# A new order for the ramp, products of zeros in its gaps, and six steps moved behind attention steps

## The chip, the cores and the metric

The kernel runs on one core of a Trainium2 chip. Its engines are TensorE (PE in the profile, with its weight loads as PEld), VectorE (DVE), ScalarE (ACT), GpSimd (POOL) and the queue of SyncE (SP), which issues nearly all DMAs. The metric is the device time of one execution in microseconds. Kernel before: 889.75 us, the median of three runs (886.77, 889.75 and 893.33).

## What is computed

Three layers follow each other on 3,072 tokens of 512 features: chunked attention, a gated two-matrix layer, and a layer with softmax and layer norm. The weights of the two later layers come as float64.

```python
# attention: 32 queries see 16 left, 32 own, 8 right keys and 8 memory keys
scores = scale * np.matmul(q_c, k_full.transpose(0, 1, 3, 2))
scores = scores - np.max(scores, axis=-1, keepdims=True)
a = np.exp(scores)
a = a / (np.sum(a, axis=-1, keepdims=True) + 1e-09)
out[:, :, c_start:c_end] = np.matmul(a, v_full)
# layer 1
x = (x @ w_a) * (x @ w_b) @ w_out
# layer 2
h = x @ w_in
e = np.exp(h - h_max)
solu = h * e / (np.sum(e, axis=-1, keepdims=True) + 1e-09)
return (solu - mu) / np.sqrt(var + 1e-06) * g_ln @ w_out
```

## The kernel before

**Products.** Each operand of the large products is kept as two parts, a high one rounded to the fast float32 format of TensorE and a low one with the rest; a product is then three products (`mm3`, lines 857 to 859) of 128x512. The attention's own products (64-row pieces, 64 or 32 columns) are plain float32.

**Attention groups.** 128 queries of all eight heads are one group, in eight steps: P makes the tile `s` (two of the eight banks of PSUM), S (line 194) is the product of queries and keys, 64 small products in the trace; M (205, 206) takes off the row maximum on DVE; X (214) is the exponential on ACT into `EB`; N (222 to 225) normalises, in the first stage on DVE; T (235) transposes on TensorE into `pt`, and a copy on ACT (237) brings that into `AT`; V (259) multiplies with the values; a copy on ACT (273, the high part of `x`) and a subtraction on DVE, L (278, the low part), end it. Later, pairs of groups do the same in one (`pair_P` to `pair_V`, lines 304 to 372; 128 small products in S and in V).

**Weights.** A layer-1 weight column block f (f = 0 to 11) comes as float64 words (`raw`, 1.5 MB) and is turned into its two parts by seven steps: abs and low on ACT (378, 381), range and sign and add on DVE (391, 392, 399, 407), hi on ACT (410), lo on DVE (414).

**Stages.** The first 40 us, the ramp, do the four groups of the first 512 tokens and turn weight blocks 0 to 2. Then a loop over f runs block 0: two runs of 12 products (`ab`) with a copy to `G` (1323), the gate on DVE and ACT (872, 874, 878), 12 products into `acc`, and the turning of weight blocks f+1 to f+3 between them. A second loop over f runs block 1. The four blocks left go two by two with seven half-size products in place of eight; the sums of weights that this takes are made in the second loop (`s1_whole`, `s1_sums`, `s1_hi`, `s1_lo`: lines 488, 502, 513, 520, on DVE, DVE, ACT, DVE) and, for `w_out`, in the third (`wo_load` to `wo_store`: 622, 632, 636, 640, 643). Layer 2 comes last, from 410 us on.

**What sets the order.** PE, DVE and ACT run in the order in which the code is written, one instruction after the other. In the ramp that is the list of calls at lines 1237 to 1291. In the first loop it is `plan`, whose numbers name a place ("9b" is behind the gate of f = 9; 31 is behind `gate_lo` of f = 10). In the second and third it is a clock: `at(t, step)` puts a step behind the `tick()` number t, six products apart, and steps of one tick run in the order in which they were registered, attention pairs first. `ps_at` holds one tile of two banks, so S of a group waits for X of the one before, and V for the copy of `pt`.

Of the kernel before, what the change touches and what calls it, by code (L numbers as in the profile page):

```python
# [8 lines left out]
F32 = mybir.dt.float32  # L9
# [46 lines left out]
def fused_kernel(  # L56
# [111 lines left out]
    def att_P(qi):  # L168
        full = ps_at.tile([P, 2, 512], F32, tag="at", name="s")
        s = full[:, :, 0:NP * CK].rearrange("q r (p k) -> q r p k", p=NP)  # L170
        if qi % NG == 0:
            nc.vector.memset(s[0:CQ, :, :, 0:16], NEG)
        if qi % NG == NG - 1:

            zero = ident[GQ - CQ:GQ, 0:8 * H].rearrange("q (r p k) -> q r p k", r=2, p=NP)
            nc.scalar.activation(
                out=s[GQ - CQ:GQ, :, :, 56:64], in_=zero, func=AF.Copy, scale=0.0, bias=NEG
            )
        quads[qi]["s"] = s

    def att_S(qi):

# [27 lines left out]
    def att_X(qi):  # L210
        st = quads[qi]
        s = st.pop("s")
        e = EB[:, next_of("e", 2)].rearrange("q (p r k) -> q p r k", p=NP, r=2)
# [15 lines left out]
    def att_T(qi, pool=None, tag=None):  # L229

        st = quads[qi]
        e = st["e"].rearrange("q (p r) k -> q p (r k)", r=2)
        pt = (pool or ps_at).tile([P, NP, GQ], F32, tag=tag or "at", name="pt")
        for p in range(NP):
            nc.tensor.transpose(pt[:, p, :], e[:, p, :], ident)
        at = AT.rearrange("q (p t) -> q p t", p=NP)
        nc.scalar.copy(at, pt)
        st["at"] = at

    def att_V(qi, pool=None, tag=None):  # L240

# [30 lines left out]
        for rs, px in parts:  # L272
            nc.scalar.copy(xh[:, rs], px)  # L273
        rest[qi] = [(px, xh[:, rs], xl[:, rs]) for rs, px in parts]

    def att_L(qi):
        for px, xh, xl in rest.pop(qi):
# [67 lines left out]
            nc.tensor.transpose(pt[:, p, :], e[:, p, :], ident)  # L345
        nc.scalar.copy(EB.rearrange("q g (p t) -> q (g p) t", p=NP), pt)

    def pair_V(d):

        full = ps_at.tile([P, 2, 512], F32, tag="at", name="px")  # L350
        px = full.rearrange("d r (o g t) -> d r o g t", o=2, g=2)
        for i in range(2):
            v = quads.pop(2 * d + i)["v"]
            at = EB[:, i].rearrange("q (p t) -> q p t", p=NP)
            for c in range(NCH):
                t = slice(CQ * c, CQ * c + CQ)
                for p in range(NP):
                    half = 64 * (p % 2)
                    for r in range(2):
                        rows = slice(64 * r, 64 * r + 64)  # L360
                        nc.tensor.matmul(  # L361
                            px[half:half + 64, r, p // 2, i, t],
                            v[rows, c, p, :],
                            at[rows, p, t],
                            start=True,
                            stop=True,
                        )
# [853 lines left out]
    make_identity(nc, ident)  # L1221
    nc.vector.memset(mhalf, -0.5)
    nc.vector.memset(zero1, 0.0)
    warm = sm_p.tile([P, 1], F32, tag="warm", name="warm")
    nc.scalar.activation(out=warm, in_=mhalf, func=AF.Exp)

    def N(i):
        att_N(i, nc.vector)
# [5 lines left out]
        att_V(i, ps_acc, "acc")  # L1234


    att_P(0)
    att_S(0)
    att_M(0)
    w1_abs(0, 0)  # L1240
    att_X(0)
    w1_range(0, 0)
    w1_abs(0, 1)
    att_P(1)
    att_S(1)
    N(0)
    T(0)
    att_M(1)
    w1_range(0, 1)
    w1_abs(0, 2)  # L1250
    att_X(1)
    att_P(2)
    att_S(2)
    w1_range(0, 2)
    w1_low(0)
    V(0)
    N(1)
    T(1)
    att_M(2)
    w1_sign(0)  # L1260
    att_L(0)
    att_X(2)
    att_P(3)
    att_S(3)
    V(1)
    N(2)
    T(2)
    att_M(3)
    w1_add(0)
    att_L(1)  # L1270
    att_X(3)
    w1_hi(0)
    V(2)
    N(3)
    w1_abs(1)
    T(3)
    w1_lo(0)
    att_L(2)
    w1_range(1)
    V(3)  # L1280
    w1_low(1)
    att_L(3)
    w1_sign(1)
    w1_abs(2)
# [117 lines left out]
    for t, fn, i in ((41, x1_hi, 0), (44, x1_lo, 0), (46, x1_hi, 1), (48, x1_lo, 1)):  # L1402
        at(t, fn, i)
    for q in range(NF1):
        for k, fn in zip(
            ((0, 2, 5, 7), (7, 8, 10, 12), (13, 14, 16, 19))[q % 3], (s1_whole, s1_sums, s1_hi, s1_lo)
        ):
            at(16 * (q // 3) + k + 1, fn, q)
# [62 lines left out]
    for p, (a, b, c, d, e) in enumerate((  # L1471
# [6 lines left out]
    )):  # L1478
        for (f, k), fn in zip((a, b, c, d, e), (wo_load, wo_sums, wo_hi, wo_lo, wo_store)):
            at(when(0, f, k), fn, p)  # L1480
# [412 lines left out]
```

## Time and profile before

| | |
|---|---|
| three runs | 886.77, 889.75, 893.33 us |
| profiled execution | 887.32 us, of which the span is 885.5 us |
| PE busy in the span | 857.7 us (97%) |
| PE idle in the span | 27.8 us |
| DVE, ACT, POOL busy | 718.4, 397.7, 63.5 us |
| DMA moved | 216.08 MB, mean 244 GB/s |

The page gives busy time by engine, the span in 40 slices, the DMA queues, and the chain of work that ended last: 80% of it is PE, 11% DVE, 4% DMA. A timeline row is start, length, engine, line, operation, output<-input, shapes, and in brackets the idle time of that engine just before with what ended it. TensorE's granted clock stands as 1.00 in every window asked for, the ramp among them; its two rates are read from the distance between the starts of equal products.

### The profile page before, as it was taken

How to read it: one execution, taken by the hardware profiler on the slowest of the kernel's cores; microseconds unless marked ns; L12 is line 12 of the kernel's file. 1: busy time of each engine (PE TensorE's matmuls, PEld its weight loads, DVE VectorE, ACT ScalarE, POOL GpSimd, SP SyncE). 2: the span in 40 equal slices, each digit the busy share in tenths (PEclk: the TensorE clock that was granted, in tenths of full speed). 3: DMA queues.
4: the chain of work that ended last, by engine and by line, in shares of the span. 5: the costliest groups of instructions: out<-in, count | busy, mean ns of one | idle time of the engine just before them, and what ended most of it. 6: DMA issues, size and time to landing. Idle time of an engine off the chain costs nothing.

```text
span 885.5 us, 16775 instructions
## 1 busy us (share of the span) xinstructions
PE 857.7 (97%) x6696; PEld 708.0 (80%) x6696; DVE 718.4 (81%) x1162; ACT 397.7 (45%) x587; POOL 63.5 (7%) x77
## 2 busy tenths in 40 slices
PE   3899999999999999999999999999999999999998
PEld 3688877788887887888888888888888888888887
DVE  6999975978876665767967777998589999999892
ACT  3677643333343423334655544356354544444332
POOL 0000000000000000000000000000232222322010
PEclk9999999999999999999999999999999999999999
DMA  9995446987699888982798988648912455564344
GB/s 372 422 414 207 155 150 211 293 281 246 215 339 408 308 319 281 339 292 88 250 328 321 344 333 312 235 171 288 318 66 94 149 163 167 165 184 139 119 141 134
DMA packets 103264, 216.08 MB, mean 244 GB/s; under 512 B 8593, under 2 KB 64145, under 8 KB 97937
## 3 DMA queue, kind: packets, MB, share of 16 engines
q1 hardware_dynamic: 103152, 214.99, 69.2%
q8 instruction: 53, 0.87, 0.4%
q14 instruction: 27, 0.21, 0.1%
q0 software_dynamic: 32, 0.00, 0.0%
HBM read 147.85 MB, written 67.11 MB: 243 GB/s over the span
## 4 chain that ended last, share of the span: by engine, by line
PE 80%; DVE 11%; DMA 4%; issue 3%; ACT 1%; SPq 0%; ACTq 0%; DVEq 0%
PE acc L756 24%; PE pab L1192 15%; PE acc L970 13%; PE pab L727 7%; PE acc L727 5%; PE pab L857 2%; PE pab L858 2%; DVE Z L399 2%; PE pab L859 2%; DVE Z L407 2%; PE px L361 2%; PE s L194 2%; DMA w<-wos 2%; PE px L259 1%; PE acc L857 1%
## 5 line engine op out<-in xcount | busy, mean ns | idle before, releaser
L756 PE MATMUL acc<-w 128*128 128x512 f32 x978 | 227.5, 391 | 0.5 <-DMA w<-wsa 0.5
L756 PEld LDWEIGHTS acc<-w 128*128 128x128 f32 x978 | 182.7, 188 | 38.9 <-DMA w<-wsa 0.9
L1192 PE MATMUL pab<-w 128*128 128x512 f32 (+1 forms) x600 | 134.4, 381 | 0.0
L1192 PEld LDWEIGHTS pab<-w 128*128 128x128 f32 x600 | 109.4, 188 | 21.9 <-DVE w L1169 0.3
L857 PE MATMUL pab<-x,w 128*128 128x512 f32 (+1 forms) x200 | 78.5, 393 | 1.8 <-ACT x L273 0.9
L918 POOL TENSOR_TENSOR w2ld<-w2ld 128x256 f32<-128x256 f32 x44 | 38.9, 903 | 545.0 <-ACT r L747 496.8
L858 PE MATMUL pab<-x,w 128*128 128x512 f32 (+1 forms) x200 | 76.9, 384 | 0.1
L859 PE MATMUL pab<-x,w 128*128 128x512 f32 (+1 forms) x200 | 76.7, 384 | 0.0
L727 PE MATMUL pab<-w 128*128 128x512 f32 x288 | 70.6, 391 | 0.4 <-DMA w<-wos 0.3
L769 DVE TENSOR_TENSOR part<-acc,part 128x512 f32<-128x512 f32 x56 | 38.6, 689 | 35.0 <-PE acc L756 28.2
L727 PEld LDWEIGHTS pab<-w 128*128 128x128 f32 x288 | 53.7, 188 | 12.5 <-issue 0.8
L970 PE MATMUL acc<-w,hx 128*128 128x512 f32 x252 | 60.6, 390 | 0.1
L970 PE MATMUL acc<-w 128*128 128x512 f32 x252 | 60.3, 390 | 0.0
L970 PEld LDWEIGHTS acc<-w,hx 128*128 128x128 f32 x252 | 47.1, 188 | 10.3 <-DVE mx L986 0.5
L970 PEld LDWEIGHTS acc<-w 128*128 128x128 f32 x252 | 47.1, 188 | 9.8
L727 PE MATMUL acc<-w 128*128 128x512 f32 x216 | 51.8, 389 | 0.0
L727 PEld LDWEIGHTS acc<-w 128*128 128x128 f32 x216 | 40.5, 188 | 8.5
L857 PEld LDWEIGHTS pab<-x,w 128*128 128x128 f32 x200 | 38.0, 190 | 10.0 <-ACT raw L381 1.3
L858 PEld LDWEIGHTS pab<-x,w 128*128 128x128 f32 x200 | 37.9, 190 | 7.4 <-DVE x L278 0.4
L859 PEld LDWEIGHTS pab<-x,w 128*128 128x128 f32 x200 | 37.9, 189 | 7.4
L702 DVE TENSOR_TENSOR w<-r,w 128x512 fp32r<-128x512 f32 x56 | 37.6, 688 | 2.1 <-ACT w L698 2.1
L857 PE MATMUL acc<-gh,w 128*128 128x512 f32 x96 | 38.1, 397 | 0.0
(236 smaller groups left out, 1404.5 us busy)
## 6 DMA issues: line engine op xcount, KB each, us to landing
w<-wsa SPq DMA_DIRECT2D x24, 1024.0 KB, 6.7
w<-wsb SPq DMA_DIRECT2D x24, 768.0 KB, 6.1
raw<-w1d_dram SPq DMA_DIRECT2D x11, 1536.0 KB, 21.4
qk<-qkv_dram SPq DMA_DIRECT2D x20, 640.0 KB, 6.0
w<-wos SPq DMA_DIRECT2D x48, 256.0 KB, 4.5
ztd<-r SPq DMA_DIRECT2D x84, 128.0 KB, 2.3
v<-qkv_dram SPq DMA_DIRECT2D x20, 512.0 KB, 4.9
r<-ztd SPq DMA_DIRECT2D x20, 512.0 KB, 3.9
```

The source lines that it names most:

```text
L194: nc.tensor.matmul(s[CQ * c:CQ * c + CQ, r, p, lo:hi], st["q"][rows, p, CQ * c:CQ * c + CQ], st["k"][rows, p, k0 + lo:k0 + hi], start=True ...
L361: nc.tensor.matmul(px[half:half + 64, r, p // 2, i, t], v[rows, c, p, :], at[rows, p, t], start=True, stop=True,)
L702: nc.vector.tensor_tensor(out=c[:, 1], in0=op_src(k), in1=c[:, 0].bitcast(F32), op=ALU.subtract)
L727: nc.tensor.matmul(ps, w[:, u, sl], g[:, v], start=first and n == 0, stop=last and n == 2, skip_group_check=True,)
L756: nc.tensor.matmul(ps, w[:, u, k], xx[v][:, k], start=(start and k == 0 and i == 0), stop=(stop and k == 1 and i == 2), skip_group_check=True,
L769: nc.vector.tensor_tensor(out=o, in0=a, in1=b, op=op)
L857: nc.tensor.matmul(ps, wl, xh, start=first, stop=False)
L858: nc.tensor.matmul(ps, wh, xl, start=False, stop=False)
L859: nc.tensor.matmul(ps, wh, xh, start=False, stop=last)
L918: (nc.gpsimd if j else nc.vector).tensor_tensor(out=s4[:, i], in0=a, in1=b, op=op)
L970: nc.tensor.matmul(ps, x, y, start=(start and k == 0 and i == 0), stop=(stop and k == 1 and i == 2), skip_group_check=True,)
L1192: nc.tensor.matmul(po, s[x][:, f], wo2(f)[:, h, sl], start=(m == 0), stop=(m == 3 * NF2 - 1))
```

## The change

Line numbers in the after part are those of the new file, where everything behind line 180 has moved by 10 to 62 lines.

1. The ramp. The list of calls has a new order. The load of the third group's queries and keys is put ahead of the values of the first two, and the load of weight block 1 ahead of the values of the fourth. T of these four groups writes `pt` to the banks `ps0` and `ps1`, which the loop uses later, and its copy (`att_A`) goes back into the group's own half of `EB`, not into `AT`, as a step of its own; the copy behind V is a step of its own too (`att_C`).
2. Products of zeros. `busy(n, cols)` issues n products of a tile of zeros with itself into the part of the tile `s` that no score uses: 28 of 32x16 and 59 of 128x256, 87 in all, in nine places of the ramp. DVE fills the zeros (128x256) first.
3. Six steps elsewhere. T of the fifth group moves from place 31 to "10a", ahead of the gate of f = 10; the four `s1` steps of q = 0 and the `s1_hi` and `s1_lo` of q = 6 move behind steps of attention pairs; `wo_lo` and `wo_store` of p = 2 move from (4,6) and (5,1) to (5,1) and (5,3); V of pair 9 is cut in two halves with six products between.

```diff
+    def busy(n, cols):
+        for _ in range(n):
+            nc.tensor.matmul(
+                spare_bank["at"][0:min(P, 2 * cols), 0:cols],
+                zeros[:, 0:min(P, 2 * cols)], zeros[:, 0:cols], start=True, stop=True,
+            )
...
-        at = AT.rearrange("q (p t) -> q p t", p=NP)
-        nc.scalar.copy(at, pt)
+        if tag in (None, "acc"):
+            at = AT.rearrange("q (p t) -> q p t", p=NP)
+            nc.scalar.copy(at, pt)
+        else:
+            at = st["eb"].rearrange("q (p t) -> q p t", p=NP)
+            st["pt"] = pt
...
+    def att_A(qi):
+        st = quads[qi]
+        nc.scalar.copy(st["at"], st["pt"])
...
+    values.append(att_load(2, s0 + 2))
     values[0]()
     values[1]()
-    for i in range(2, n0):
-        values.append(att_load(i, s0 + i))
-    for i in range(2, n0):
-        values[i]()
+    values.append(att_load(3, s0 + 3))
+    values[2]()
     w1_load(1)
+    values[3]()
...
+    w1_abs(0, 0)
     att_P(0)
+    busy(28, 16)
+    busy(6, 256)
     att_S(0)
+    busy(12, 256)
     att_M(0)
...
-        (24, 24, "8a", "8a", "9b", 31, 32, 32),
+        (24, 24, "8a", "8a", "9b", "10a", 32, 32),
...
+            if fn is pair_V and d == d0 + 5:
+                at(k, pair_V0, d)
+                k += 1
+                fn = pair_V2
...
+        if q == 0:
+            places = 3, 4, 9, 10
+        elif q == 6:
+            places = 1, 3, 8, 9
...
-        ((2, 4), (4, 2), (4, 4), (4, 6), (5, 1)),
+        ((2, 4), (4, 2), (4, 4), (5, 1), (5, 3)),
```

PE at the start of the program, before, from the end of S of the first group to T of the second (`s<-qkv` is S, 32 instructions of the program each, and the first row holds the last 6 of the first group and all of the second; `pt` is T, `px` is V):

```order
L194 MATMUL s<-qkv 32x48 x2
L194 MATMUL s<-qkv 32x64 x38
L235 MATMUL pt<-ident,EB 128x128 x4
L194 MATMUL s<-qkv 32x64 x32
L259 MATMUL px<-AT,qkv 64x32 x32
L235 MATMUL pt<-ident,EB 128x128 x4
```

and now the same stretch; ahead of it, as the first rows of PE, stand the 28 and 6 products of zeros:

```order
L204 MATMUL s<-qkv 32x48 x2
L204 MATMUL s<-qkv 32x64 x6
L186 MATMUL s<-zeros 128x256 x12
L204 MATMUL s<-qkv 32x64 x32
L186 MATMUL s<-zeros 128x256 x5
L246 MATMUL pt<-ident,EB 128x128 x4
L186 MATMUL s<-zeros 128x256 x6
L204 MATMUL s<-qkv 32x64 x32
L186 MATMUL s<-zeros 128x256 x10
L278 MATMUL px<-EB,qkv 64x32 x32
L246 MATMUL pt<-ident,EB 128x128 x4
```

Zeros stand behind each of the first three S. They write the tile `s`, and the built program lets M of the groups 0, 1 and 2 on DVE wait for the last of the 12, 5 and 10 that stand behind their S, and X of the groups 1 and 3 for the 6 behind T(0) and T(2).

DVE at the first attention pair of the second loop, before (line 323 is M, 488 is `s1_whole` of q = 0, 872 the gate, 334 to 337 N, 502 `s1_sums`, 878 `gate_lo`):

```order
L323 TENSOR_TENSOR s<-s,mx 128x1024
L488 TENSOR_TENSOR Z<-w 128x1024
L872 TENSOR_TENSOR G_147<-G_147,pab 128x512
L334 TENSOR_REDUCE sm<-EB 128x16
L335 TENSOR_SCALAR sm<-sm 128x16
L336 RECIPROCAL sm<-sm 128x16
L337 TENSOR_TENSOR EB<-EB,sm 128x1024
L502 TENSOR_TENSOR Z<-Z 128x256 x4
L878 TENSOR_TENSOR gh<-G_147,gh 128x512
```

and now:

```order
L346 TENSOR_TENSOR s<-s,mx 128x1024
L907 TENSOR_TENSOR G_147<-G_147,pab 128x512
L357 TENSOR_REDUCE sm<-EB 128x16
L358 TENSOR_SCALAR sm<-sm 128x16
L359 RECIPROCAL sm<-sm 128x16
L360 TENSOR_TENSOR EB<-EB,sm 128x1024
L523 TENSOR_TENSOR Z<-w 128x1024
L913 TENSOR_TENSOR gh<-G_147,gh 128x512
L537 TENSOR_TENSOR Z<-Z 128x256 x4
```

`s1_whole` went from ahead of N to behind it, and `s1_sums` from ahead of `gate_lo` to behind it.

ACT at the fifth group's T in the first loop, before (`G_147<-pab` is the copy of f = 10, `gh` its gate, `AT<-pt` the copy of T):

```order
L410 CAST w<-Z 128x3x512
L1323 COPY G_147<-pab 128x512
L874 CAST gh<-G_147 128x512
L237 COPY AT<-pt 128x512
L273 CAST x<-px 128x2x2x128
```

and now:

```order
L445 CAST w<-Z 128x3x512
L1378 COPY G_147<-pab 128x512
L249 COPY AT<-pt 128x512
L909 CAST gh<-G_147 128x512
L297 CAST x<-px 128x2x2x128
```

The copy of T now stands ahead of the gate. On PE nothing moved here.

## Rows read from the trace of the kernel before

**Rows 1.** From the page: busy time by engine, and the instruction queue.
```profile
PE 857.7 (97%) x6696; PEld 708.0 (80%) x6696; DVE 718.4 (81%) x1162; ACT 397.7 (45%) x587; POOL 63.5 (7%) x77
q8 instruction: 53, 0.87, 0.4%
```

**Rows 2.** Busy time by engine in one stretch, the first loop.
```profile
41.20:130.00 88.80, 87.99 (x567) 72.22 (x568) 84.92 (x81) 57.41 (x54) 2.09 (x2) 1.00 0.66 243
```

**Rows 3.** Timeline of DVE in the ramp: the five instructions that waited.
```profile
5.92 0.69 DVE L205 TENSOR_REDUCE mx<-s 128x8 f32<-128x512 f32 x1 [4.84 <-PE s L194]
...
12.38 0.43 DVE L391 TENSOR_SCALAR Z<-Z 128x512 f32<-128x512 f32 x1 [0.34 <-ACT Z L378]
...
16.85 0.69 DVE L205 TENSOR_REDUCE mx<-s 128x8 f32<-128x512 f32 x1 [1.82 <-PE s L194]
...
20.92 0.69 DVE L222 TENSOR_REDUCE sm<-EB 128x8 f32<-128x512 f32 x1 [0.33 <-ACT EB L214]
...
33.21 0.76 DVE L278 TENSOR_TENSOR x<-px,x 128x256 fp32r<-128x256 f32 x2 [0.61 <-ACT x L273]
```

**Rows 4.** Busy time of DVE from its first M to the end of lo(1).
```profile
5.92:41.05 35.13, 31.06 (x49) 1.00 1.02 422
```

**Rows 5.** Timeline of PE: products at its two rates, and the last wait of the ramp.
```profile
24.22 1.11 PE L235 MATMUL pt<-ident,EB 128*128 128x128 f32 x4
...
35.56 0.63 PE L859 MATMUL pab<-x,w 128*128 128x512 f32 x1
35.98 0.46 PE L857 MATMUL pab<-x,w 128*128 128x512 f32 x1
36.28 0.39 PE L858 MATMUL pab<-x,w 128*128 128x512 f32 x1
36.51 0.40 PE L859 MATMUL pab<-x,w 128*128 128x512 f32 x1
...
41.20 0.47 PE L857 MATMUL pab<-x,w 128*128 128x512 f32 x1 [0.86 <-DVE w L414]
```

**Rows 6.** Timeline at T and V of the fifth group.
```profile
122.22 0.60 PE L235 MATMUL pt<-ident,EB 128*128 128x128 f32 x4
...
125.77 0.58 ACT L237 COPY AT<-pt 128x512 f32<-128x512 f32 x1
...
126.40 1.13 PE L259 MATMUL px<-AT,v 64*64 64x32 f32 x64 [0.81 <-ACT AT L237]
```

**Rows 7.** Timeline at the first attention pair, `s1` steps of q = 0.
```profile
155.75 1.22 DVE L488 TENSOR_TENSOR Z<-w 128x1024 f32<-128x1024 f32 x1
155.88 1.03 ACT L329 ACTIVATE EB<-s 128x1024 f32<-128x1024 f32 x1 [1.09 <-DVE s L323]
...
157.48 1.22 DVE L334 TENSOR_REDUCE sm<-EB 128x16 f32<-128x1024 f32 x1
...
160.60 1.06 PE L345 MATMUL pt<-ident,EB 128*128 128x128 f32 x8 [0.89 <-DVE EB L337]
...
162.20 1.05 ACT L513 CAST Z<-Z 128x1024 fp32r<-128x1024 f32 x1 [3.98 <-DVE Z L502]
...
164.70 2.07 PE L361 MATMUL px<-EB,v 64*64 64x32 f32 x128 [0.29 <-ACT EB L346]
```

**Rows 8.** Timeline at the third attention pair, `s1_hi` of q = 6.
```profile
215.93 1.05 ACT L513 CAST Z<-Z 128x1024 fp32r<-128x1024 f32 x1 [5.18 <-DVE G L872]
...
218.46 2.07 PE L361 MATMUL px<-EB,v 64*64 64x32 f32 x128 [0.63 <-ACT EB L346]
```

**Rows 9.** Timeline at T of pair 9, and the next copy on ACT behind `wo_hi`.
```profile
334.12 1.06 PE L345 MATMUL pt<-ident,EB 128*128 128x128 f32 x8 [0.78 <-DVE EB L337]
...
347.00 0.59 ACT L1617 COPY part<-acc 128x512 f32<-128x512 f32 x1 [3.70 <-PE acc L756]
```

**Rows 10.** Timeline of PE: the two gaps inside runs of small products.
```profile
152.80 0.45 PE L194 MATMUL s<-qk 64*32 64x64 f32 x30 [0.64 <-issue]
...
340.82 0.48 PE L361 MATMUL px<-EB,v 64*64 64x32 f32 x18 [1.13 <-issue]
```

More of the change, by code (lines that the diff above doesn't have):

```diff
@@ L179, in att_P @@
         quads[qi]["s"] = s
+        spare_bank["at"] = full[:, 0, NP * CK:]
+    spare_bank = {}
+    def busy(n, cols):
[4 more added lines that the diff above has]
+            )
     def att_S(qi):
@@ L212, in att_X @@
         s = st.pop("s")
-        e = EB[:, next_of("e", 2)].rearrange("q (p r k) -> q p r k", p=NP, r=2)
+        st["eb"] = EB[:, next_of("e", 2)]
+        e = st["eb"].rearrange("q (p r k) -> q p r k", p=NP, r=2)
         nc.scalar.activation(
@@ L271, in att_V, with att_C @@
         )
-        for rs, px in parts:
-            nc.scalar.copy(xh[:, rs], px)
         rest[qi] = [(px, xh[:, rs], xl[:, rs]) for rs, px in parts]
+        if qi >= 4:
+            att_C(qi)
+    def att_C(qi):
+        for px, xh, xl in rest[qi]:
+            nc.scalar.copy(xh, px)
     def att_L(qi):
@@ L346, in pair_T, with pair_V0, pair_V1, pair_V2 @@
         nc.scalar.copy(EB.rearrange("q g (p t) -> q (g p) t", p=NP), pt)
+    def pair_V0(d):
+        full = ps_at.tile([P, 2, 512], F32, tag="at", name="px")
+        pairs[d]["px"] = full
+        pair_V1(d, 0)
     def pair_V(d):
-        full = ps_at.tile([P, 2, 512], F32, tag="at", name="px")
+        pair_V0(d)
+        pair_V2(d)
+    def pair_V1(d, i):
+        full = pairs[d]["px"]
         px = full.rearrange("d r (o g t) -> d r o g t", o=2, g=2)
[L352 to L367, printed above, removed]
+        v = quads.pop(2 * d + i)["v"]
+        at = EB[:, i].rearrange("q (p t) -> q p t", p=NP)
+        for c in range(NCH):
+            t = slice(CQ * c, CQ * c + CQ)
+            for p in range(NP):
+                half = 64 * (p % 2)
+                for r in range(2):
+                    rows = slice(64 * r, 64 * r + 64)
+                    nc.tensor.matmul(
+                        px[half:half + 64, r, p // 2, i, t],
+                        v[rows, c, p, :],
+                        at[rows, p, t],
+                        start=True,
+                        stop=True,
+                    )
+    def pair_V2(d):
+        pair_V1(d, 1)
+        full = pairs[d].pop("px")
         bi, off = d // 2, d % 2 * 2 * GQ
@@ L1223, in fused_kernel @@
     nc.vector.memset(zero1, 0.0)
+    zeros = g_tile(1, F32R, "zeros")
+    nc.vector.memset(zeros[:, 0:256].bitcast(F32), 0.0)
     warm = sm_p.tile([P, 1], F32, tag="warm", name="warm")
@@ L1234, in V @@
         att_V(i, ps_acc, "acc")
+    w1_abs(0, 0)
     att_P(0)
+    busy(28, 16)
+    busy(6, 256)
     att_S(0)
+    busy(12, 256)
     att_M(0)
-    w1_abs(0, 0)
     att_X(0)
@@ L1243, in fused_kernel @@
     w1_abs(0, 1)
+    w1_abs(0, 2)
+    N(0)
     att_P(1)
     att_S(1)
-    N(0)
-    T(0)
+    busy(5, 256)
     att_M(1)
+    att_T(0, ps_ab, "ps0")
+    busy(6, 256)
+    w1_range(0, 2)
+    att_X(1)
+    att_A(0)
     w1_range(0, 1)
-    w1_abs(0, 2)
-    att_X(1)
     att_P(2)
     att_S(2)
-    w1_range(0, 2)
+    busy(10, 256)
+    N(1)
+    V(0)
     w1_low(0)
-    V(0)
-    N(1)
-    T(1)
     att_M(2)
+    att_T(1, ps_ab, "ps1")
+    att_X(2)
     w1_sign(0)
-    att_L(0)
-    att_X(2)
     att_P(3)
     att_S(3)
-    V(1)
-    N(2)
-    T(2)
-    att_M(3)
-    w1_add(0)
-    att_L(1)
[L1271 to L1276, printed above, removed]
+    att_A(1)
+    att_C(0)
+    N(2)
+    att_M(3)
+    V(1)
+    att_C(1)
+    att_T(2, ps_ab, "ps0")
+    busy(6, 256)
+    att_L(0)
+    att_X(3)
+    att_A(2)
+    w1_abs(1)
+    V(2)
+    busy(5, 256)
+    w1_add(0)
+    N(3)
+    w1_hi(0)
+    att_C(2)
+    att_T(3, ps_ab, "ps1")
+    busy(5, 256)
+    att_A(3)
+    att_L(1)
+    V(3)
+    busy(4, 256)
+    w1_range(1)
+    w1_low(1)
     w1_lo(0)
+    att_C(3)
     att_L(2)
-    w1_range(1)
-    V(3)
-    w1_low(1)
     att_L(3)
@@ L1392, in pair @@
                     at(k, pair_load, d + 1, 0, False)
-            if fn is pair_V and d % 4 < 3:
+            if fn in (pair_V, pair_V2) and d % 4 < 3:
                 at(k, pair_load, d + 1, 1, False)
@@ L1404, in fused_kernel @@
     for q in range(NF1):
[L1405 to L1408, printed above, removed]
+        places = ((1, 3, 6, 8), (8, 9, 11, 13), (14, 15, 17, 20))[q % 3]
+        if q == 0:
+            places = 3, 4, 9, 10
+        elif q == 6:
+            places = 1, 3, 8, 9
+        for k, fn in zip(places, (s1_whole, s1_sums, s1_hi, s1_lo)):
+            at(16 * (q // 3) + k, fn, q)
     for t, fn, i in (
```

## The prediction

> **What bounds the kernel now.** I read the page first: PE is busy for 857.7 of 885.5 us [rows 1], so whatever the change does away from PE counts only where PE waits, and all idle time of PE is 27.8 us. Next the busy times by stretch: over the first loop PE is busy for 87.99 of 88.80 us and DVE for 84.92 [rows 2]. PE is the bound there, but DVE is close behind it, so a ramp that ends earlier on PE alone gives nothing; the weights that DVE turns must be early too. Then the timeline of the ramp, where most of the idle time lies. DVE is its spine: from its first M at 5.92 to the end of lo(1) at 41.05 it is busy for 31.06 of 35.13 us [rows 4], and PE's last wait of the ramp, 0.86 us at 41.20, is for that lo [rows 5]. From 41.20 on PE hardly waits. So the ramp is worth as much as lo(1) comes earlier. DVE's own waits inside that stretch are four: 0.34, 1.82, 0.33 and 0.61, together 3.10 us; the 1.82 is for S of the third group, whose data come last [rows 3]. That is the most a new order can give. Behind the ramp I went to each gap of PE that the change touches [rows 6 to 10].
>
> **The ramp's order.** DVE runs the same instructions before and after, apart from the fill of the zeros, which ends while it waits for data anyway (4.84 us idle, [rows 3]). The new order takes away the cause of each of the four waits: the third group's queries and keys are loaded ahead of two values, its abs of the second third goes ahead, L of each group comes later, and the last C is followed by other work. Gain up to 3.10 us.
>
> **The zeros.** The first M now waits for the 12 products of zeros behind its S. PE has two rates in this trace. Until 35.98 products of 512 columns start 0.42 us apart (35.56 to 35.98), that is 1.2 GHz, and from 36.28 on 0.23 apart (36.28 to 36.51), that is 2.4 GHz [rows 5]; the granted clock reads 1.00 at both places, so I go by the distances. A zero of 256 columns costs half of that, 0.21 at the low rate and 0.12 at the high one. Twelve cost 2.5 or 1.4 us, with about 0.2 for the last to drain: the first M starts at 8.6 or 7.5 in place of 5.92, 2.7 or 1.6 us late. Behind it DVE has work without a break up to the third M, which now waits for ten zeros (2.1 or 1.2 us); by then DVE has caught up to within 0.4 us of them, so I add 0 to 0.4. The ramp's net is -3.10 + 1.6 = -1.5 us if the rate is high from the start of the twelve, and -3.10 + 2.7 + 0.4 = 0.0 if it rises only behind them. Before, the rate rose at 36, inside the program's first run of long products, which began 2.8 us earlier, with the last L at 33.2 [rows 3, 5]; here the first long zeros can start at about 3 us (an estimate: 1.5 for the fills and 1.5 for the small ones), with S of the first group between them and the twelve, so the rise should fall inside the twelve. I take the middle, -0.7. What the high rate saves in T (1.11 us at 24.22 against 0.60 at 122.22, [rows 5, 6]) lies beside DVE's work and counts only in so far as it keeps DVE fed. The 28 small zeros and the six long ones behind them must end by 4.7, when the first data land; if each small one took as long as a long one at the low rate they would end 2.7 us late, and since the nearest rows are small attention products at 0.015 each (30 in 0.45, [rows 10]) I take 0.
>
> **T of the fifth group.** PE waits 0.81 us for the copy of T, which ACT starts at 125.77, although T was through at 122.82 [rows 6]: the gate stands ahead of it. With the gate behind it ACT copies at once, while PE has 12 products to do. Gain 0.8. The copy takes 0.58 on ACT, within the 2.95 us between T's end and the place where it ran; if the gate behind it were ready by then it would lose that 0.58, to an x2 step that is 12 products away.
>
> **First pair, q = 0.** `s1_whole` (1.22 us) runs from 155.75, and N starts at 157.48, behind the gate. Without it N starts when X ends, 155.88 + 1.03 = 156.91, so 0.57 earlier, and PE's 0.89 before T shrinks to 0.3. `s1_hi` on ACT waited 3.98 us for `s1_sums` and held the copies behind it; behind the pair's copy it no longer does, and PE's 0.29 at 164.70 goes [rows 7]. Gain 0.57 + 0.29 = 0.85. The sums are late by two places, which only their stores see.
>
> **Third pair, q = 6.** `s1_hi` stands on ACT for 1.05 us in front of the copy for which PE waits 0.63 at 218.46 [rows 8]. Gain 0.6.
>
> **Pair 9, p = 2.** `wo_lo` stands in front of N on DVE (1,024 columns, as long as the `s1_whole` of [rows 7], 1.22 us), and PE waits 0.78 for N [rows 9]. Gain 0.8. The store of p = 2 goes out some 5 us later, and the next `wo_hi` on ACT must wait for it; the ring load behind it on SP's queue is late by 2 us. Both have room: the copy that is next on ACT comes behind 3.70 us of idle time [rows 9], and the load is for a block of weights two turns of the loop on. I cost it at 0; with that cover gone, PE would wait for the copy by what the store is late.
>
> **Pair 9's V, and the first pair's S.** PE stands still for 1.13 and 0.64 us inside an unbroken run of 128 small products, waiting for nothing that the profile shows [rows 10]. The instruction queue moved 0.87 MB in 53 packets, 16.4 KB each, and PE ran 2 x 6,696 products and weight loads [rows 1]: 253 instructions a packet. Counted in the program with packets of 256, both gaps lie 98 products behind the start of a packet, with nothing but small products in between: PE had used up a packet before the next was there. Cutting V in two puts six long products (1.4 us) into it, and the 87 zeros move every packet's start by about 174 instructions, so both gaps go: 1.8 us. Three other runs now have a packet's start within their first 18 products (V of pair 5, S of pair 9, S of pair 11). Before, five did and two of them had a gap. I let one come back, 0.9: net gain 0.9, bounds -0.9 (all three come back) and 1.8. The Trainium skill's page "Runtime: NRT & Kernel Launch" (section "Instruction fetch mechanics") has instructions fetched in blocks of 256 while the block before runs, and calls the cost of crossing a block mostly hidden; by it this term would be 0. The two rows speak against it: 1.77 us were not hidden.
>
> **Sum.** 0.7 + 0.8 + 0.85 + 0.6 + 0.8 + 0.9 = 4.65 us. Against the profiled execution's own time, 887.32, that is 882.7; this execution lies 2.4 us under the median of the three runs, on which the same gain gives 885.1. I forecast between the two, **884 us**. All terms lie on PE's path, and DVE, ACT and the queues behind have the same lead as before, so they add up.
>
> **Rivals.** (a) *The clock falls back in the ramp's gaps.* By the steps above PE stands idle for some 2 us behind the twelve zeros, waiting for X of the first group, and for near 1 us at each later T; and T took 1.11 us in a stretch in which PE was already busy most of the time [rows 5], so small products do not keep the rate up. Then the ten zeros cost 2.1 us, the third M starts 2 us later than in the forecast, and the ramp's term turns from -0.7 to +1.3: gain 2.6. The Trainium skill's page "TensorE: Matmul & The Clock Gate" (section "What's actually happening") calls the low rate the default that activity releases; whether zeros in gaps hold it no row here shows. (b) *The packets' gaps return* at all three places: gain 4.65 - 1.8 = 2.8. (c) *The zeros work as a brake, slower than before.* If PE keeps the low rate until the long products come, the twelve, five, six and ten each hold M, X or S for their full price, and V and T keep their long times in a chain that is now tighter: 2.7 us at the first M, 0.5 at the second (five zeros at 0.21 for 0.12), 1.1 at the third (ten, and S) and some 2.3 in the T and V behind them, which then take 0.5 and more each beyond their short times, less 3.1: the ramp ends 3.5 us later. That leaves a gain of 0.5. At 0.24 a zero and a late first S (0.9) it is a loss of 0.8. It turns to slower as soon as the ramp ends over 3.95 us later than now. (d) *The six moves do nothing*, because the next wait in line takes each place (the gate for N, the copy of G for hi): then 0.7 is left. Against it: in each place the row shows the moved step directly in front of the one that PE waits for.
>
> **Chances.** Forecast 0.55, (a) 0.16, (b) 0.11, (c) 0.08, (d) 0.06, and 0.04 for more than is counted, a high rate from the first zeros on and no gap back (-1.5 and 1.8: gain 6.4 and more). The range takes in the ramp at -1.5 with no gap back on the profiled basis (880.9) and case (a) or (b) on the median (887), and stops short of no change at 889.75: 880 to 889. All runs of before lie within 0.4% of their median, and 1% (8.9 us) is about what a measurement of this kernel can tell from no change; no case reaches it: faster by over 1% 0.04, within 1% 0.94, slower 0.02.
>
> **What would show it.** Ramp: the first M on DVE at 7.5 to 8.6, no wait of over 0.5 us on DVE behind it, lo(1) done at about 40.4, PE's T at 0.6. Moves: PE's waits at the fifth V, the first pair's T and V, the third pair's V and pair 9's T gone or under 0.4. Packets: no "issue" gap in V of pair 9 or S of pair 4, perhaps one in V of pair 5 or S of pair 9 or 11. The forecast is wrong if PE's T in the ramp still takes 1.1, if lo(1) ends behind 42, or if new waits for DVE stand in the first loop.

## The result and the profile after

The changed kernel takes 895.16 us (median of four runs, 894.30 to 895.79), the kernel before, run beside it, 888.26 (885.40 to 893.33): a ratio of 1.0075, with a 95% interval of 1.0053 to 1.0098. It is 6.7 us slower; 884 was forecast, 4 to 6 us faster. The profiled executions, on which the reading rests, lie 8.4 us apart (895.77 and 887.32).

Busy time by engine from the page after, beside [rows 1]:

```profile
PE 873.6 (98%) x6783; PEld 721.4 (81%) x6783; DVE 719.2 (80%) x1163; ACT 398.0 (45%) x587; POOL 63.5 (7%) x77
```

PE is busy for 15.9 us more and idle for 20.4 us in place of 27.8. So the change did take away waits; what it added is busy time, the zeros and products that run at a lower rate. To see where, the start of the same piece of work on PE is compared in the two traces (timelines of PE). Pairs are counted in order of time; the first is pair 4 of the code, the sixth pair 9:

| piece of work on PE | before | after | later by |
|---|---|---|---|
| second run of `ab` in the first loop (first needs lo(1)) | 41.20 | 45.06 | 3.86 |
| S of the fifth group | 101.26 | 106.72 | 5.46 |
| T of the fifth group | 122.22 | 127.74 | 5.52 |
| V of the fifth group | 126.40 | 131.02 | 4.62 |
| S of the first pair (`s1` of q = 0) | 150.94 | 155.61 | 4.67 |
| V of the first pair | 164.70 | 168.29 | 3.59 |
| S of the second pair | 175.10 | 178.68 | 3.58 |
| T of the second pair | 187.53 | 193.09 | 5.56 |
| V of the second pair | 191.25 | 198.96 | 7.71 |
| T of the third pair (`s1_hi` of q = 6) | 214.05 | 221.97 | 7.92 |
| V of the third pair | 218.46 | 225.69 | 7.23 |
| V of the fourth pair | 245.03 | 253.28 | 8.25 |
| V of the fifth pair | 299.51 | 309.10 | 9.59 |
| T of pair 9 | 334.12 | 342.80 | 8.68 |
| S of the pair behind it | 355.06 | 362.71 | 7.65 |
| V of that pair | 375.33 | 382.95 | 7.62 |
| S of the last pair | 384.36 | 393.08 | 8.72 |
| end of the span | 885.5 | 894.0 | 8.5 |

Two places make the loss: the ramp with what follows it (5.5 us) and the stretch from the second pair's S to its V (4.1 us). Between them most of the moved steps give what was forecast.

**The ramp.** Timeline of PE, of DVE and of ACT after (line 186 is a product of zeros, 204 S, 215 M, 225 X, 449 lo, 892 a product of `ab`; in brackets the idle time before and what ended it), beside [rows 3] and [rows 5]:

```profile
5.84 2.93 PE L186 MATMUL s<-zeros 128*128 128x256 f32 x12
8.80 0.69 DVE L215 TENSOR_REDUCE mx<-s 128x8 f32<-128x512 f32 x1 [7.43 <-PE s L186]
10.98 0.86 PE L204 MATMUL s<-qkv 64*32 64x64 f32 x64 [2.21 <-ACT EB L225]
14.24 1.65 PE L186 MATMUL s<-zeros 128*128 128x256 f32 x6 [0.20 <-DVE s L216]
15.93 0.60 ACT L225 ACTIVATE EB<-s 128x512 f32<-128x512 f32 x1 [3.86 <-PE s L186]
17.69 2.50 PE L186 MATMUL s<-zeros 128*128 128x256 f32 x10
20.23 0.69 DVE L215 TENSOR_REDUCE mx<-s 128x8 f32<-128x512 f32 x1 [1.81 <-PE s L186]
43.16 1.75 DVE L449 TENSOR_TENSOR w<-Z,w 128x1536 fp32r<-128x1536 f32 x1
43.33 1.62 ACT L416 ACTIVATE raw<-raw 128x1536 int32<-128x1536 uint32 x1
45.06 0.47 PE L892 MATMUL pab<-x,w 128*128 128x512 f32 x1 [1.89 <-ACT raw L416]
46.91 0.63 PE L893 MATMUL pab<-x,w 128*128 128x512 f32 x1
47.34 0.63 PE L894 MATMUL pab<-x,w 128*128 128x512 f32 x1
```

Each of the three waits that end with `PE s L186` is a step that stands still until zeros are through: the first M at 8.80 in place of 5.92 (most of its 7.43 is the wait for data, which stood before as well), X of the second group at 15.93, the third M at 20.23. lo(1) starts at 43.16 (39.30 before). The 1.89 us of PE at 45.06 are put down to L416, a step on ACT that writes `raw`, which no product reads; lo(1) ends 0.04 us ahead of it, at 44.91, and is what that product reads.

Busy times by stretch after (start:end, length, busy time of PE, PEld, DVE, ACT, POOL with their instructions, PE's granted clock, DMA share, GB/s), cut where the granted clock changes:

```profile
5.84:8.77 2.93, 2.92 (x16) 2.63 (x12) 0.00 (x0) 0.67 (x1) 0.00 (x0) 1.00 1.00 405
8.96:12.38 3.42, 1.40 (x69) 1.31 (x69) 3.25 (x8) 1.74 (x3) 0.00 (x0) 1.00 1.02 414
20.12:27.20 7.08, 7.08 (x203) 6.45 (x203) 6.73 (x12) 2.38 (x6) 0.00 (x0) 0.50 1.03 426
36.27:46.51 10.24, 8.35 (x63) 6.52 (x60) 9.27 (x9) 7.20 (x7) 0.00 (x0) 1.00 1.00 416
46.51:49.92 3.41, 3.41 (x10) 2.64 (x9) 3.41 (x5) 1.73 (x3) 0.00 (x0) 0.50 1.06 434
```

The twelve zeros take 0.24 each, the low rate (1.2 GHz), though the column reads 1.00 there, as it does up to the trace's first recorded change of the clock. At 8.96, just behind them, the rate did rise (S at 10.98 takes 0.86 in place of 1.17); but PE was busy for only 1.40 of the 3.42 us that follow, and at 12.38 the clock fell to 0.50. There it stayed until 36.27, through stretches in which PE was busy all the time with zeros, transposes and small products (20.12 to 27.20). At 46.51, behind PE's 1.89 us of waiting for lo(1), it fell again until 49.92: from 46.51 to 49.90 eight products take 3.39 us, some 0.43 each, where the distance at the high rate is 0.23 [rows 5]. That is 1.55 us, and the table steps from 3.86 to 5.46.

**Behind the first pair.** The chain of waits after, in order of time (start, length, what); line 548 is `s1_hi`, 542 and 543 its and `s1_lo`'s stores, 316 and 312 loads of a later pair's queries, keys and values, 523 `s1_whole`, 907 the gate:

```profile
170.14 0.96 ACT Z L548
171.12 0.36 SPq L542
171.53 0.46 SPq L543
172.08 0.45 SPq L316
172.62 0.39 SPq L312
173.56 6.76 DMA wsb<-Z
180.44 0.17 DVE Z L523
183.48 0.60 DVE G L907
```

The wait on DVE and PE's waits behind it, from the timelines, and then the busy times of five of the 8.2 us in which SP's queue issued nothing:

```profile
180.44 1.23 DVE L523 TENSOR_TENSOR Z<-w 128x1024 f32<-128x1024 f32 x1 [3.76 <-DMA wsb<-Z]
190.46 0.50 PE L892 MATMUL pab<-x,w 128*128 128x512 f32 x1 [0.57 <-ACT G L1485]
193.09 1.06 PE L368 MATMUL pt<-ident,EB 128*128 128x128 f32 x8 [0.97 <-DVE EB L360]
196.44 0.50 PE L892 MATMUL pab<-x,w 128*128 128x512 f32 x1 [0.90 <-DVE G L907]
198.96 1.25 PE L392 MATMUL px<-EB,v 64*64 64x32 f32 x72 [0.85 <-ACT EB L369]
```

```profile
165.00:170.00 5.00, 5.00 (x134) 4.23 (x136) 4.86 (x10) 1.98 (x3) 0.00 (x0) 1.00 0.07 26
```

`s1_hi` of q = 0 now runs at 170.1 (162.20 before, [rows 7]), and its store is the next entry of SP's queue. Until it could go, SP issued nothing from 162.9 to 171.1, and from 165 to 170 the DMA engines moved 26 GB/s. All that stood behind (the next pair's loads, the stores of `s1_lo`, those of `wo`) then came at once; the store of `s1_lo` took 6.76 us to land, `s1_whole` of a later q waited 3.76 us on DVE for the half of `Z` that it frees, and two gates and the second pair's M and N stood behind it on DVE. PE felt it four times, 3.3 us. The table has 4.1, since the modelled ends make each wait look short: products of 512 columns start 0.23 apart and are shown 0.39 long.

**Gaps behind packets of instructions.** The gaps of [rows 10] are gone, and three others have come; timeline of PE after, with the runs of small products ahead of two of them:

```profile
159.41 0.39 PE L893 MATMUL pab<-x,w 128*128 128x256 f32 x1 [0.92 <-issue]
...
287.84 1.48 PE L204 MATMUL s<-qk 64*32 64x64 f32 x128
292.31 3.92 PE L791 MATMUL acc<-w 128*128 128x512 f32 x16 [0.73 <-issue]
...
382.95 2.07 PE L392 MATMUL px<-EB,v 64*64 64x32 f32 x128
386.30 3.90 PE L791 MATMUL acc<-w 128*128 128x512 f32 x16 [0.85 <-issue]
```

Counted in the program, packets begin 41, 40 and 32 products into the small runs ahead; 87, 88 and 96 small products and 10, 9 and 1 long ones later PE stands still: 97 each time. The two gaps before lie 97 products behind the start of a packet as well (the 98 that the prediction counts take in the packet's first). The traces bear this out for every kernel here: the timelines of the 14 kernels put 38 waits of PE down to `issue` (0.16 to 2.66 us), and counted over all of TensorE's recorded instructions (weight loads, products, semaphores) 35 of them stand behind instruction 193 of 256, the others behind 194, 195 and 196.

### The profile page after: what moved, and what is told of

It reads as the page before. It is cut to its first block, busy times and chain, and to the rows that moved or that the text cites. A ratio compares the mean times of both kernels' runs of the same rounds, so it can differ in the third digit from the quotient of the medians.

```text
span 894.0 us, 16953 instructions
## 1 busy us (share of the span) xinstructions
PE 873.6 (98%) x6783; PEld 721.4 (81%) x6783; DVE 719.2 (80%) x1163; ACT 398.0 (45%) x587; POOL 63.5 (7%) x77
## 4 chain that ended last, share of the span: by engine, by line
PE 86%; DVE 7%; DMA 3%; ACT 2%; issue 1%; SPq 1%; ACTq 0%; DVEq 0%
PE acc L791 25%; PE pab L1227 15%; PE acc L1005 13%; PE pab L762 7%; PE acc L762 5%; PE pab L892 3%; PE pab L893 3%; PE pab L894 3%; DMA wsb<-Z 2%; PE acc L892 2%; PE acc L893 2%; PE s L204 2%; PE acc L894 2%; PE px L392 1%; PE px L278 1%
```

## The experiments

Each ratio is to the kernel before, measured beside it; its median there was 887.2 to 888.7. All edits are to the changed kernel where nothing else is said.

| kernel | median, us | ratio and 95% interval | lo(1) starts |
|---|---|---|---|
| changed | 895.16 | 1.0075 (1.0053 to 1.0098) | 43.16 |
| no_zeros | 887.51 | 1.0001 (0.9990 to 1.0011) | 36.95 |
| q0_back | 891.26 | 1.0047 (1.0030 to 1.0063) | 42.73 |
| free_zeros | 890.75 | 1.0039 (1.0021 to 1.0057) | 39.46 |
| hold12 | 889.19 | 1.0014 (0.9995 to 1.0032) | 39.51 |
| early_zeros | 887.69 | 0.9997 (0.9981 to 1.0013) | 38.31 |
| no_zeros_no_s1 | 882.08 | 0.9947 (0.9928 to 0.9967) | 35.93 |
| best1 | 882.68 | 0.9930 (0.9905 to 0.9956) | 36.90 |
| q0_middle | 883.53 | 0.9937 (0.9914 to 0.9959) | 35.94 |
| whole_V | 883.03 | 0.9940 (0.9919 to 0.9962) | 36.52 |
| q9_too | 883.59 | 0.9946 (0.9929 to 0.9964) | 36.30 |
| ramp_only | 884.75 | 0.9974 (0.9951 to 0.9997) | 35.95 |

### Without the zeros

```diff
     def busy(n, cols):
-        for _ in range(n):
+        for _ in range(0):
```

> The changed kernel without its 87 products of zeros and without their fill; the new ramp order and the six moves stay. Theory 1 (the zeros hold M and X and so brake the ramp): the first M on DVE is back at 5.9, PE's second run of ab starts at 38 to 40 (45.06 with zeros, 41.20 in the kernel before), no stretch at half clock behind 46; the time falls by 6 to 8 us to 887 to 889. Rival 1 (the new order is at fault): the second run of ab starts at 43 to 45 and the time stays within 1.5 us of 895.2. The instruction packets shift back by 174 instructions, so single gaps of about 1 us may come and go; they are read from the trace and not counted for either.

By the ratios the time falls by 0.74%, 6.6 us, to that of the kernel before. lo(1) starts at 36.95, 6.2 us earlier, and the second run of `ab` at 39.15, 2.05 before the 41.20 of the old order, with no wait and no half clock behind it. Theory 1 holds; the new order is not at fault. What the order gains is lost again behind the first pair, where the wait of the changed kernel stands, now 5.04 us, with PE's four waits behind it (0.60, 0.96, 0.90 and 0.86; timeline of DVE of no_zeros):

```profile
36.95 1.75 DVE L449 TENSOR_TENSOR w<-Z,w 128x1536 fp32r<-128x1536 f32 x1
174.65 1.23 DVE L523 TENSOR_TENSOR Z<-w 128x1024 f32<-128x1024 f32 x1 [5.04 <-DMA wsb<-Z]
```

### The new order by itself

The kernel before with the new list of calls and of loads alone, without zeros and without the six moves; against the changed kernel, beside the zeros:

```diff
-        (24, 24, "8a", "8a", "9b", "10a", 32, 32),
+        (24, 24, "8a", "8a", "9b", 31, 32, 32),
...
-            if fn is pair_V and d == d0 + 5:
-                at(k, pair_V0, d)
-                k += 1
-                fn = pair_V2
...
-        ((2, 4), (4, 2), (4, 4), (5, 1), (5, 3)),
+        ((2, 4), (4, 2), (4, 4), (4, 6), (5, 1)),
```

> The kernel before with the new order of the ramp alone, without products of zeros and without the six moves. The step of the forecast that takes away DVE's four waits: lo(1) begins at 36 to 37 (39.30 before), PE's second run of ab at 38 to 39, time 2.3 to 3.4 us under the kernel before. The waits of [rows 6 to 9] and the two gaps of [rows 10] stand as before, the gaps at nearly the same products, since only two instructions of PE are gone. Rival (what the ramp gains is lost in the first loop, where DVE is nearly as busy as PE): time within 1 us of the kernel before.

2.3 us faster, with lo(1) at 35.95 and the second run of `ab` at 38.32: at the lower edge of what theory 1 gave. Not all of the 2.9 us in the ramp shows in the time; at 215.96 PE now waits 1.68 us for the copy at which it waited 0.63 before [rows 8], and the granted clock is 0.50 from 216.76 to 223.58 (no such stretch before):

```profile
215.96 3.02 PE L392 MATMUL px<-EB,v 64*64 64x32 f32 x128 [1.68 <-ACT EB L369]
216.76:223.58 6.82, 6.82 (x99) 5.79 (x92) 4.07 (x7) 2.63 (x4) 0.00 (x0) 0.50 0.75 261
```

### Zeros that nobody waits for

```diff
-        spare_bank["at"] = full[:, 0, NP * CK:]
+    def zbank(tag):
+        spare_bank["at"] = ps_ab.tile([P, TB], F32, tag=tag, name="zb")
...
     att_P(0)
+    zbank("ps1")
     busy(28, 16)
...
     att_T(2, ps_ab, "ps0")
+    zbank("ps1")
     busy(6, 256)
...
     att_T(3, ps_ab, "ps1")
+    zbank("ps0")
     busy(5, 256)
```

> The changed kernel with all 87 products of zeros at their places on PE, but written to the tiles of ps0 and ps1 in place of s, so that M and X no longer wait for them. Theory 1 in its narrow form (the waiting of M and X is the loss): first M at 5.9, second run of ab at 37.5 to 40, time 887 to 889, as without zeros. Rival 3 (the zeros cost by the time they take on PE and by a half clock that follows them): second run of ab at 42 or later, time over 891.5. If the clock now stays high from the first zeros on, T in the ramp takes 0.6 in place of 1.1 and the second run starts at about 37.4.

It lies between the two theories: 890.75, and the second run of `ab` at 41.36. The first M is back at 6.13, and lo(1) starts at 39.46, 3.7 us earlier than with the zeros in `s`, but 2.5 later than without them. And here the rate did rise early: it is high from 7.87 to 21.52, and T of the first group takes 0.63. That bought nothing, since lo(1) is late all the same. Timeline of PE (line 206 is S, 248 T, 280 V) and of DVE (303 is L):

```profile
10.29 0.63 PE L248 MATMUL pt<-ident,EB 128*128 128x128 f32 x4 [0.20 <-DVE EB L238]
20.15 0.71 PE L206 MATMUL s<-qkv 64*32 64x64 f32 x47 [2.14 <-issue]
26.26 1.11 PE L280 MATMUL px<-EB,qkv 64*64 64x32 f32 x58 [1.41 <-issue]
32.69 0.36 PE L280 MATMUL px<-EB,qkv 64*64 64x32 f32 x9 [0.76 <-issue]
33.47 0.76 DVE L303 TENSOR_TENSOR x<-px,x 128x256 fp32r<-128x256 f32 x2 [2.12 <-ACT x L299]
```

PE stands still three times, 4.3 us together, waiting for nothing that the profile shows, and DVE then waits 2.12 for what comes behind. no_zeros has one such gap in its ramp, 2.00 us at 21.92, and DVE waits nowhere behind it.

### Twelve zeros alone, and the early ones alone

Two kernels that keep a part of the calls of `busy`. hold12 keeps the twelve:

```diff
     att_P(0)
-    busy(28, 16)
-    busy(6, 256)
     att_S(0)
     busy(12, 256)
...
-    busy(5, 256)
...
-    busy(6, 256)
```

and so on for all behind it. early_zeros has it the other way round, with the two calls ahead of `att_S(0)` and no other.

> The changed kernel with only the 12 products of zeros behind S of the first group, the other 75 left out. Theory 1: the first M starts 2.7 to 3 us late (8.7 to 8.9), and as DVE waits little behind it, lo(1) begins 1.5 to 2.5 us later than without zeros (35.93 to 36.95 there), at 38 to 39.5; time 1.5 to 2.5 us over that of the kernel without zeros, 889 to 890.5. Rival (DVE makes up for it at its later waits for data): lo(1) at 36 to 37.3 and no difference to it.

> The changed kernel with only the first 34 products of zeros (28 small, 6 long), which stand ahead of the first data; the 53 behind steps of attention are left out. Theory 1 (zeros cost where a step waits for them, and by their own time between steps): these cost nothing, first M at 5.9 to 6.2, lo(1) begins at 36 to 37.5 as without zeros (36.95), time 885.5 to 889.5 by where the instruction packets fall. Rival (zeros from the start on are enough to raise the rate of PE early): T of the first two groups takes 0.6 to 0.7 in place of 1.1 and lo(1) begins at 35 to 36.

With the twelve, the first M starts at 8.89 and lo(1) at 39.51, 2.6 us and more later than without zeros; in the time it is 1.2 us, which the intervals do not separate from no_zeros. The early zeros hold no step and leave the time as it was without zeros, and the rate rose only at 38.1; but against the expectation they were not free in the ramp: lo(1) came 1.4 us later than in no_zeros, by a gap in S of the fourth group, for which DVE's M then waited (timelines of PE and DVE of early_zeros):

```profile
21.11 0.46 PE L204 MATMUL s<-qkv 64*32 64x64 f32 x13 [2.66 <-issue]
21.65 0.69 DVE L215 TENSOR_REDUCE mx<-s 128x8 f32<-128x512 f32 x1 [2.07 <-PE s L204]
```

### The s1 steps of q = 0

q0_back takes them back to their old places; q0_middle leaves the zeros out and moves two of them by one place:

```diff
-        if q == 0:
-            places = 3, 4, 9, 10
-        elif q == 6:
+        if q == 6:
```

```diff
-            places = 3, 4, 9, 10
+            places = 3, 4, 8, 9
```

> The changed kernel with the four s1 steps of q = 0 at their old places (ticks 1, 3, 6, 8), all else as changed. Theory 2 (the late s1 steps send their stores late, s1_whole of a later q waits on DVE for such a store, and gates and the second pair queue behind it): DVE's waits of 3.76 and 1.59 us for stores of Z go, PE's waits of 0.57, 0.97, 0.90 and 0.85 at 190 to 199 go, PE's 0.89 in front of T of the first pair comes back; the time falls by 3 to 4 us to 891 to 892. Rival 2 (the DMA traffic there is late for another reason, as the ramp's 4 us of delay): these waits stay and the time stays within 1 us of 895.2.

> The changed kernel without products of zeros and with s1_hi and s1_lo of q = 0 one tick earlier, (3, 4, 8, 9) in place of (3, 4, 9, 10). Theory 2 (the late sending of the stores is the cost): the stores leave some 2 us earlier, DVE's longest wait for a store of Z falls from 5.0 (in the kernel without zeros) to 2 to 3.5, and the time falls by 1 to 2.5 us from 887.5 to 885 to 886.5. Rival (the queue of DMAs in front of the stores decides when they land, whenever they are sent): the wait stays at 4 to 5 us and the time within 0.7 us of 887.5.

q0_back: 3.9 us less between the medians, as theory 2 gave, but 2.5 by the ratios, whose intervals overlap; PE's four waits at 190 to 199 are gone. The 0.89 ahead of T of the first pair did not come back: PE was itself 0.65 late there by a gap of instructions. In its profiled execution the clock did not fall behind the ramp, although PE waited 1.90 us there too, so part of the difference of the two traces is not the steps'. q0_middle settles it without that: against no_zeros, from which it differs by one place of two steps, it is 0.64% faster, 5.7 us, more than was expected (4.0 between the medians; the kernel before, beside them, had 887.2 and 888.7). In the two traces 5.3 us of it arise in one stretch, from S of the second pair (171.50 in no_zeros, 170.03 in q0_middle) to S of the third (203.55 and 196.75). `s1_hi` now goes right behind the pair's copy on ACT, SP issues its store at 160.31, and `s1_whole` waits for no store there (three of them on DVE, and the entries of SP's queue):

```profile
159.12 1.22 DVE L523 TENSOR_TENSOR Z<-w 128x1024 f32<-128x1024 f32 x1
166.31 1.22 DVE L523 TENSOR_TENSOR Z<-w 128x1024 f32<-128x1024 f32 x1
174.56 1.22 DVE L523 TENSOR_TENSOR Z<-w 128x1024 f32<-128x1024 f32 x1
...
160.31 0.36 SPq L542 DMA_DIRECT2D wsa<-Z  x1
162.52 0.46 SPq L543 DMA_DIRECT2D wsb<-Z  x1
```

### Both causes away, and q = 6 and q = 9

no_zeros_no_s1 leaves out the zeros and moves the `s1` steps of q = 0 and q = 6 back (first diff); best1 keeps the move of q = 6, as q0_back does; q9_too moves q = 9 like q = 6, on q0_middle (second diff).

```diff
-        if q == 0:
-            places = 3, 4, 9, 10
-        elif q == 6:
-            places = 1, 3, 8, 9
```

```diff
-        elif q == 6:
+        elif q in (6, 9):
```

> The changed kernel without the products of zeros and with the s1 steps of q = 0 and q = 6 at their old places; what is left is the new ramp order, T of the fifth group, the moved wo_lo and wo_store and V of pair 9 in two halves. Theories 1 and 2 together: the losses add, so the time is 10 to 12 us below the changed kernel, 883 to 885.5, that is 3 to 5 us below the kernel before (888.3). If either theory is wrong it stays above 888.

> The changed kernel without products of zeros and with the s1 steps of q = 0 at their old places; unlike no_zeros_no_s1 it keeps the move of s1_hi and s1_lo of q = 6. In no_zeros_no_s1 (882.1 us) PE waits 1.58 us for the copy of EB at 215.10 with that move undone, and V behind it takes 2.65 in place of 2.07. Theory (the move of q = 6 does what was forecast): this wait goes and the time falls by 1.5 to 2 us to 880 to 880.7. Rival (its late stores cost on DVE what it gains, as those of q = 0 do): new waits of DVE for stores of Z of over 1.5 us behind 218 and a wait of PE of about 1 us at V of the next pair; time 881.5 to 882.5.

> The kernel q0_middle with s1_hi and s1_lo of q = 9 moved in the same way as those of q = 6, behind the pair's copy of EB. In q0_middle PE waits 0.61 us for that copy at 240.13. If it works as at q = 6 without late stores the wait goes and the time falls by 0.5 us, too little to be told from q0_middle (0.9937 of the kernel before); if the stores come late as those of q = 0 did, DVE waits over 3 us for them and the time rises by 1 to 3 us.

The losses add: 882.08, 4.7 us below the kernel before, 13 below the changed one (11.4 by the ratios). For q = 6 nothing is decided. best1 has no wait of PE at V of the third pair (1.58 us in no_zeros_no_s1), but 3.5 us of DVE waits for stores of `Z` in place of 1.1, and 0.57 of PE at the fourth pair's V, which no_zeros_no_s1 has not; their ratios overlap. q9_too is no better than q0_middle: the wait at 240 is gone, and DVE waits up to 3.1 us for stores of `Z`. PE also waits 1.44 us at 188.91 in q9_too and 0.80 at 188.77 in whole_V, where q0_middle has no wait although the three run the same instructions up to there: one trace alone can't weigh waits of this size. I would keep q0_middle or no_zeros_no_s1; all five kernels without zeros and without the late stores of q = 0 lie at 0.9930 to 0.9947, and these runs can't order them.

### Where the packets of instructions begin

pad8 is the kernel before with eight small products more, ahead of the first data (one execution, 888.16 us, which says nothing about the time). whole_V is q0_middle with V of pair 9 in one piece (the four lines of ramp_only's diff that begin with `if fn is pair_V` taken out).

```diff
         quads[qi]["s"] = s
+        if qi == 0:
+            for _ in range(8):
+                nc.tensor.matmul(
+                    full[0:32, 0, NP * CK:NP * CK + 16], zeros[:, 0:32], zeros[:, 0:16],
+                    start=True, stop=True,
+                )
```

> The kernel before with 8 small products of zeros (32x16) more on PE, ahead of S of the first group, where PE waits for data for 4.7 us: nothing changes but that all later instructions of PE stand 16 places further on. Theory 3 (a gap comes 98 products behind the start of a packet of 256 instructions): the gap in V of pair 9 (1.13 us after 110 products) stands after 102 products of it, 0.8 to 1.4 us long; the one in S of the fourth pair (0.64 after 98) would stand after 90, and as its packet now begins among long products it is under 0.3 or gone. Rival (the gaps belong to these places of the program): they stay after 110 and 98 products.

> The kernel q0_middle with V of pair 9 in one piece. A packet of 256 instructions starts 12 products into that V. Theory 3: with V in one piece a gap of 0.7 to 1.2 us comes back behind its product 109 or 110, and the time is about 1 us over that of q0_middle (0.9937 of the kernel before), 0.994 to 0.996. Rival (the gap went for another reason, as a lighter load of DMAs): no gap, same time.

Timeline of PE of pad8 (line 200 is S of the first pair of the second loop, which the prediction and the expectation call pair 4 and fourth, 367 V of pair 9), beside [rows 10], then of ramp_only and of whole_V at the same V:

```profile
151.32 1.12 PE L200 MATMUL s<-qk 64*32 64x64 f32 x91
152.78 0.63 PE L200 MATMUL s<-qk 64*32 64x64 f32 x37 [0.33 <-issue]
337.21 1.71 PE L367 MATMUL px<-EB,v 64*64 64x32 f32 x103
339.66 0.59 PE L367 MATMUL px<-EB,v 64*64 64x32 f32 x25 [0.74 <-issue]
```

```profile
338.20 1.82 PE L392 MATMUL px<-EB,v 64*64 64x32 f32 x109
340.37 0.53 PE L392 MATMUL px<-EB,v 64*64 64x32 f32 x19 [0.34 <-issue]
```

```profile
334.00 2.07 PE L392 MATMUL px<-EB,v 64*64 64x32 f32 x128
```

The place is as theory 3 has it: both gaps moved with the packets, by seven products (eight were put in), to 103 from 110 and to 91 from 98, and stand again 97 behind the start of one. The size is not. With the packet beginning 12 or 13 products into the same V, the gap was 1.13 in the kernel before, 0.34 in ramp_only, and in whole_V there was none, with the time of q0_middle. So the cut of V is not what made the gap go, and it is worth nothing that these runs can show. What sets the size was not tried by itself; the longest gaps (2.66, 2.14, 2.00) all lie in the ramp, where the DMA share is about 1.0 throughout.

## Why the prediction was wrong, and where it was right

**The order** (up to 3.10 us): right. In the seven kernels with this order and no zeros lo(1) starts 2.4 to 3.4 us earlier than before (39.30), and PE's second run of `ab` in ramp_only and no_zeros at 38.32 and 39.15 without a wait.

**The zeros** (+1.6 to +2.7, "I take the middle"): the step that failed first. "The rise should fall inside the twelve" was wrong: it came behind them, at 8.96, and was lost at 12.38; the first M at 8.80 lies where the low rate was forecast to put it (8.6). So every later zero cost its low-rate price, and X and the third M stood still for them as case (c) had worked out: a ramp 3.5 us late there, 3.86 measured. The sum had no price for X, behind which DVE waited 0.79 us at 16.56. Case (c) had 0.08. The text held what spoke for it: T at 1.11 in a stretch in which PE is mostly busy [rows 5]. The Trainium skill's page "TensorE: Matmul & The Clock Gate" (section "What's actually happening") has activity release the clock; at 8.96 the trace agrees, but from 20.12 to 27.20 PE was busy all the time at 0.50, and in free_zeros the high rate, where it was had, did not bring lo(1) forward. Of the zeros' 6.2 us at lo(1), 3.7 are waits of M and X (free_zeros); the other 2.5 are left when nobody waits, where gaps of 4.3 us stand on PE (2.0 in no_zeros). That these gaps are the cause of the 2.5 is not shown by a run of its own. Not in the sum at all was the clock's fall behind the ramp, 1.6 us in this execution.

**First pair, q = 0** (0.85): the second step that failed. The gain came: T and V of that pair have no wait. The cost was put at nothing by "the sums are late by two places, which only their stores see". SP sends in order, so the next pair's loads, the other stores and `wo` saw it too, and through `Z` DVE did. The loss is 4.1 us on PE in the trace, and 4.0 (medians) to 5.7 us (ratios) between no_zeros and q0_middle.

**T of the fifth group** (0.8): right, 0.90 in the table. **Third pair** (0.6): 0.69 there; but 0.94 comes back at V of the next pair. **Pair 9's T** (0.8): right, 0.91.

**Packets** (0.9): the place was right, the count of gaps wrong. The two old ones went (0.64 and 1.13), three came (0.92, 0.73, 0.85), none at the three places named: I looked for them only inside runs of small products, and they fell into the first long products behind. So the term was +0.7 us and not -0.9. Case (b) had three come back, but elsewhere. The Trainium skill's page "Runtime: NRT & Kernel Launch" (section "Instruction fetch mechanics") calls the cost of crossing a block mostly hidden; of some 50 crossings here most are, but in each kernel one to six are not, at 0.2 to 2.7 us each.

**Sum.** Forecast -4.65. Measured on PE: +5.5 (ramp and clock), -0.9 (T), -1.0 (first pair with its two gaps), +4.3 (second pair, up to the third pair's T), -0.7 (V of the third pair), +1.0 (V of the fourth), +1.3 (a wait of 0.73 for a copy and the gap at 292), -0.9 (pair 9's T), -1.0 (its V), +1.1 (gap at 386), -0.2 (rest): +8.5. Two terms that were thought worth -1.55 cost +8.8 together.

## What to carry to other kernels

A step that is moved takes its DMAs with it, and in an in-order queue everything behind them: look at what stands behind the first late store, and at which buffer it frees, before the cost is put at nothing. Work that fills idle time must write where nobody reads, or it is a wait; and if the engine that it keeps warm isn't the one that sets the pace, a higher rate buys nothing, as in free_zeros. Where the DMA engines were full, runs of small products stood still for 2.0 us without zeros and 4.3 us with them (no_zeros, free_zeros): added products have to be counted against the packets too.

## What was not expected of the hardware

- The granted clock's column reads 1.00 from the start of a trace until the first change that is recorded (36.11 in the kernel before), though products run at the low rate; the distance of equal products tells it.
- The same ramp gave different clocks in two executions (best1: no change until 36.70; no_zeros: high at 19.43, 0.50 from 22.84 to 36.50), with lo(1) at 36.90 and 36.95: without zeros this difference of the clock did not show in lo(1).
- The clock fell in mid-kernel behind waits of 1.6 to 1.9 us (46.51 after; 216 in ramp_only and no_zeros_no_s1), but not behind each such wait (1.90 in q0_back, 1.80 in free_zeros). In hold12, whole_V and q9_too it fell at 149.51, 146.32 and 146.83, behind two waits of 0.73 and some 0.47 us that stand in every kernel here.
- PE stood still for up to 2.66 us at one and the same place in a packet, and at most packets not at all.
